# Windowed attention with a gated MLP: two heads' scores in one two-bank tile, and one conditional copy for both

## The chip, the core and the metric

The kernel runs on one core of one Trainium2 chip. The metric is device time in microseconds (us), lower is better; the median of several executions counts. The engines are named as in the profile: PE is TensorE (matrix products and transposes), PEld its loading of weights, DVE is VectorE, ACT is ScalarE, POOL is GpSimd, and SP issues most transfers.

## What is computed

Attention with a few sink columns and a window, then a feed-forward block with a convolution of three taps along the sequence and a gate. All data are float32.

```python
def _attn_ref(q, k, v, n_sink, window):            # (4, 8, 768, 64): batch, heads, rows, head_dim
    scores = (1.0 / np.sqrt(D)) * np.matmul(q, k.transpose(0, 1, 3, 2))
    is_sink = pos[None, :] < int(n_sink)           # n_sink = 4
    rel = pos[:, None] - pos[None, :]
    in_window = (rel >= 0) & (rel < int(window))   # window = 128
    scores = np.where(is_sink | in_window, scores, -1000000000.0)
    a = np.exp(scores - np.max(scores, axis=-1, keepdims=True))
    a = a / (np.sum(a, axis=-1, keepdims=True) + 1e-09)
    return np.matmul(a, v)

def _moe_ref(x, w_in, conv_w, w_out):              # x (4, 768, 512), w_in (512, 1024), w_out (1024, 512)
    h = np.maximum(x @ w_in, 0.0)
    # conv_out: three taps along the sequence, one weight a tap and column, zeros beyond the ends
    return (h * (1.0 / (1.0 + np.exp(-conv_out)))) @ w_out
```

A row of scores has at most 128 window columns and 4 sink columns. Of the 128 rows of one tile, row r needs columns 0 to r of its own tile (the triangle) and columns r+1 to 127 of the tile to its left: together 128 columns.

## The kernel before

**Tiling.** Heads are taken in pairs: 4 batches x 4 pairs = 16 groups g. The 768 rows of a group are 6 tiles t of 128 rows. A step is one tile of one group for both heads j, so there are 96 steps. `banded` (L398) lays the steps out in a list and writes them as a software pipeline: at position i it writes the scores of step i (`scores`, L488), the transposes of step i-1 (`transp`, L526) and, on the third tile of a half, the product with the values (`pv`, L558) of step i-2. Between them it writes pieces of the MLP of the batch before (`fill`) and the preparation of coming keys and queries (`todo`). The first 24 steps, batch 0, multiply in plain float32 (L339); the later ones in two passes of a faster format, a main part and a remainder of the keys (L342, L343).

**The MLP.** It runs in 96 units, 24 a batch. A unit has 12 matmuls into `ph` (L183: 4 blocks of the model width x 3 products), a gate on ACT, DVE and POOL (L190 to L201), and 6 matmuls into `po` (L210). The MLP of a batch needs the attention of all its heads for the rows it takes.

**Order.** The program is built with `schedule_with_timeline_sim=True` (L807): the framework decides from the dependencies, by a plan of its own, in which order each engine gets its instructions. An engine then takes them strictly in that order, so an instruction that waits holds up all those behind it on the same engine.

**A step's scores.** A score tile has 260 columns: 0 to 127 the tile to the left, 128 to 131 the sink columns, 132 to 259 the step's own tile (`P` = 128, `KW` = 132, `SW` = 260). For t = 0 only the last 128 are made. The steps on it:

- PE writes the scores of head 0 into one tile and of head 1 into another (L501 to L505). Both have the tag `sc` with two buffers, one PSUM bank each: head 0's next tile takes the first bank that is free again.
- For t > 0 DVE copies, head by head, the left neighbour's columns over those of the own tile that lie beyond the triangle (L508, a copy under the mask `before`, in place within the bank).
- DVE adds the mask over 132 columns, keeps the row's minimum (the scores are negated) in `sm`, and writes to SBUF (L509, shown as a custom operation and a read of its accumulator). With that the bank is free.
- ACT takes the exponential and its sum, head by head (L512); DVE adds up the sums of both heads (L514) and inverts them (L515); POOL scales (L517). Then PE transposes (L532).

All eight PSUM banks are taken: `h` two, `po` two, `sc` two, `px` one, `pts` one.

Of the kernel before, what the change touches and what calls it, by code (L numbers as in the profile page):

```python
# [10 lines left out]
F32 = mybir.dt.float32  # L11
F32R = mybir.dt.float32r
I32 = mybir.dt.int32
# [4 lines left out]
P = 128  # L18
# [5 lines left out]
KW = P + NS  # L24
SW = 2 * P + NS
# [372 lines left out]
def banded(c):  # L398

    nc = c.nc  # L400
# [6 lines left out]
    ap, ps = A.ap, A.ps  # L407
# [11 lines left out]
    before = cp.tile([P, P], F32, name="before")  # L419
# [64 lines left out]
            asked[0] += 1  # L484

    pts = ps.tile([P, 2, 2, P], F32, name="pts")

    def scores(g, t):  # L488
        s = st[g]
        lo = 0 if t == 0 else (t - 1) * KW  # L490
        mk = m0 if t == 0 else (m1 if t == 1 else m2)
        cols = slice(NS if t == 0 else 0, KW)
        sm = sms[A.tiles % len(sms)]
        A.tiles += 1
        hf, u = divmod(t, 3)
        if u == 0:
            s.pe[hf] = ap.tile([P, 3, 2, KW], F32, tag="pe", name=f"pe{g}_{hf}")
            if t == 0:
                nc.gpsimd.memset(s.pe[hf][:, 0, :, 0:NS], 0.0)
        pe = s.pe[hf][:, u]  # L500
        pcs = [ps.tile([P, SW], F32, tag="sc", name=f"sc{g}_{t}_{j}", bufs=2) for j in range(2)]  # L501
        if t == 0:
            A.scores(s, t, [pc[:, KW:SW] for pc in pcs], lo, lo + P)
        else:
            A.scores(s, t, pcs, lo, lo + SW)  # L505
        for j, pc in enumerate(pcs):
            if t:
                nc.vector.copy_predicated(pc[:, KW:SW], before.bitcast(I32), pc[:, 0:P])  # L508
            nc.vector.tensor_tensor_reduce(out=pe[:, j, cols], in0=pc[:, P:SW][:, cols], in1=mk, op0=ALU.add, op1=ALU.min,  # L509
                                           scale=1.0, scalar=3.0e38, accum_out=sm[:, j:j + 1])  # L510
        for j in range(2):
            nc.scalar.activation(pe[:, j, cols], pe[:, j, cols], AF.Exp, bias=sm[:, j:j + 1], scale=-1.0,  # L512
                                 accum_out=sm[:, 2 + 2 * j:3 + 2 * j])
        nc.vector.tensor_reduce(out=sm[:, 6:8], in_=sm[:, 2:6].rearrange("p (j e) -> p j e", e=2), op=ALU.add, axis=mybir.AxisListType.X)  # L514
        nc.vector.reciprocal(sm[:, 8:10], sm[:, 6:8])  # L515
        for j in range(2):
            nc.gpsimd.tensor_scalar(pe[:, j, cols], pe[:, j, cols], sm[:, 8 + j:9 + j], 1.0, ALU.mult, ALU.mult)  # L517
# [112 lines left out]
    for i in range(NST + D2):  # L630
        if i < NST:
            n, g, t = steps[i]
# [15 lines left out]
        for slot in range(SLOTS):  # L648
            if slot == 0 and i < NST:
                scores(g, t)  # L650
            if slot == 1 and 0 <= i - D1 < NST:
                transp(*steps[i - D1][1:])
            if slot == 2 and 0 <= i - D2 < NST:
                pv(*steps[i - D2][1:])
                if i - D2 + 1 in cuts:
                    while fill:
                        fill.pop(0)()
                    lo, hi, span = cuts[i - D2 + 1]
                    fill = m.pieces(lo, hi)
                    rate = len(fill) / (span - 0.5)  # L660
                    acc = 0.0
            acc += rate / SLOTS
            while acc >= 1.0 and fill:
                fill.pop(0)()
                acc -= 1.0
            while todo and i + (slot + 1) / SLOTS >= todo[0][0]:
                todo.pop(0)[1]()
# [73 lines left out]
def attention_gated_mlp(ctx: ExitStack, tc: tile.TileContext, q, k, v, n_sink, window, w_in, conv_w, w_out, out):  # L741
# [33 lines left out]
    with tc.If(fast == 1) as cmp:  # L775
        with ExitStack() as es:
            c.es = es
            banded(c)
# [32 lines left out]
```

## Time and profile before

| | us |
|---|---|
| median of 3 runs | 489.43 |
| lowest and highest | 487.89, 490.92 |
| the profiled execution | 490.03 |
| its span, first to last instruction | 488.3 |

The profile is of one execution. Busy time of an engine leaves out waits and the instructions that only issue transfers or handle semaphores. Matmuls are pipelined, so their durations overlap. A "group" is all instructions of one line, operation and shape, with their busy time and the mean length of one; behind it stands how long the engine had been idle before them, and what ended that. "Who waited for whom" gives the total, the number of times and the longest. The chain of waits goes back from the last instruction, at each step to what released it. In a timeline a row is start, length, engine, line, operation, output<-inputs, shapes, and a count where neighbours are merged; the time in brackets is the idle time before it and its releaser.

By span: the first 20 us load and set up, the first 24 steps run up to about 97 us, the other 72 from 100.0 to 402.5 us (L509's first and last start are 10.3 and 402.5 us), and after 412 us only the MLP of the last batch is left.

### The profile page before, as it was taken

To read this page: it belongs to the slowest core of one execution; us is meant where nothing else is said; L and a number is where in the kernel's file an instruction comes from. 1 tells how busy PE (TensorE), PEld (TensorE's weight loads), DVE (VectorE), ACT (ScalarE), POOL (GpSimd) and SP (SyncE) were. 2 spreads that over 40 slices of the span, in tenths; PEclk is the share of its full clock that TensorE was granted. 3 is DMA by queue.
4 is the path that set the end of the run, shared out by engine and by line. 5 is a ranking of instruction groups with operands and counts; after the bars stand their busy time and mean duration, and the time that the engine had idled before them with its cause. 6 is when DMAs were issued, how large, how long until landed. Compare 5 with 4: busy or idle time off the path is not lost.

```text
span 488.3 us, 10470 instructions
## 1 busy us (share of the span) xinstructions
PE 457.4 (94%) x3149; PEld 389.7 (80%) x3149; DVE 348.4 (71%) x1212; ACT 340.5 (70%) x1086; POOL 312.7 (64%) x614
## 2 busy tenths in 40 slices
PE   2887798899999999999999999999999999999995
PEld 2555477688889888888888888888888888999993
DVE  4798989957968777786677585886675665656553
ACT  3887858778878977786877786876776754545451
POOL 3584796867976867684758577685764564344441
PEclk9988989999999999999999999999999999999998
DMA  5778653537234132334132332324021100101011
GB/s 147 211 229 212 172 168 79 126 85 188 67 72 116 61 83 66 87 96 99 60 77 58 85 81 60 70 63 98 24 55 33 44 3 0 44 2 44 1 44 53
DMA packets 87307, 41.03 MB, mean 84 GB/s; under 512 B 80160, under 2 KB 80184, under 8 KB 87240
## 3 DMA queue, kind: packets, MB, share of 16 engines
q1 hardware_dynamic: 87096, 39.99, 31.5%
q8 instruction: 28, 0.46, 0.4%
q14 instruction: 39, 0.32, 0.2%
q10 hardware_dynamic: 144, 0.26, 0.2%
HBM read 27.60 MB, written 6.29 MB: 69 GB/s over the span
## 4 chain that ended last, share of the span: by engine, by line
PE 80%; DVE 7%; DMA 3%; issue 3%; ACT 2%; POOL 2%; SPq 1%; DVEq 0%; ACTq 0%; POOLq 0%
PE po L210 27%; PE ph L183 26%; PE px L573 8%; PE sc L342 4%; PE pts L532 4%; PE sc L343 3%; PE px L576 2%; PE tq L276 2%; PE tk L294 2%; PE sc L339 2%; POOL pe L517 1%; DVE sc L508 1%; DMA wi_1r<-in_moe_w_in_dram 1%; DVE pe L509 1%; DVE stm L113 1%
## 5 line engine op out<-in xcount | busy, mean ns | idle before, releaser
L210 PE MATMUL po<-woH,g 128*128 128x512 f32 x384 | 142.0, 409 | 1.2 <-POOL g L200 1.0
L183 PE MATMUL ph<-xH,wiH 128*128 128x258 f32 (+1 forms) x384 | 112.2, 292 | 1.2 <-ACT X L255 1.2
L183 PE MATMUL ph<-xH,wiL 128*128 128x258 f32 (+1 forms) x384 | 109.0, 284 | 0.0
L183 PE MATMUL ph<-xL,wiH 128*128 128x258 f32 (+1 forms) x384 | 108.8, 284 | 0.0
L517 POOL TENSOR_SCALAR pe<-pe,sm 128x132 f32<-128x132 f32 (+1 forms) x192 | 82.8, 442 | 34.9 <-DVE sm L515 27.2
L512 ACT ACTIVATE pe<-pe,sm 128x132 f32<-128x132 f32 (+1 forms) x192 | 77.5, 406 | 15.8 <-DVE sm L509 14.7
L200 POOL TENSOR_SCALAR g<-t 128x256 fp32r<-128x256 f32 x96 | 42.2, 439 | 70.7 <-DVE t L198 50.8
L195 DVE SCALAR_TENSOR_TENSOR t<-hb,cw,t 128x256 f32<-128x256 f32 x96 | 54.0, 562 | 36.6 <-ACT t L194 36.1
L201 POOL TENSOR_TENSOR g<-t,g 128x256 fp32r<-128x256 f32 x96 | 75.2, 784 | 5.6
L210 PEld LDWEIGHTS po<-woH,g 128*128 128x128 f32 x384 | 68.7, 189 | 11.6 <-POOL g L200 2.6
L183 PEld LDWEIGHTS ph<-xH,wiH 128*128 128x128 f32 x384 | 73.0, 190 | 5.5 <-ACT X L255 1.6
L210 PE MATMUL po<-woL,g 128*128 128x512 f32 x192 | 76.4, 398 | 0.0
L183 PEld LDWEIGHTS ph<-xH,wiL 128*128 128x128 f32 x384 | 72.9, 190 | 2.1
L183 PEld LDWEIGHTS ph<-xL,wiH 128*128 128x128 f32 x384 | 72.8, 190 | 0.7
L197 ACT ACTIVATE t<-t 128x256 f32<-128x256 f32 x96 | 40.1, 418 | 33.8 <-DVE t L196 33.4
L198 DVE SCALAR_TENSOR_TENSOR t<-t,hb 128x256 f32<-128x256 f32 x96 | 47.5, 494 | 20.1 <-ACT t L197 19.0
L508 DVE COPY_PREDICATED sc<-before,sc 128x128 f32<-128x128 int32 x160 | 45.6, 291 | 22.6 <-PE sc L343 19.1
L509 DVE CUSTOM_DVE_ANT_0 pe<-sc,m 128x132 f32<-128x132 f32 (+1 forms) x192 | 54.0, 288 | 10.3 <-PE sc L343 7.8
L190 ACT ACTIVATE hb<-ph 128x258 f32<-128x258 f32 (+1 forms) x96 | 37.0, 386 | 31.4 <-PE ph L183 30.7
L536 POOL TENSOR_SCALAR_AFFINE_SELECT pT<-pT 128x256 f32<-128x256 f32 x80 | 38.2, 477 | 31.4 <-ACT pT L534 31.1
L196 DVE SCALAR_TENSOR_TENSOR t<-hb,cw,t 128x256 f32<-128x256 f32 x96 | 54.1, 564 | 4.1
L194 ACT ACTIVATE t<-hb,cw 128x256 f32<-128x256 f32 x96 | 49.2, 513 | 7.7 <-POOL g L201 3.9
(124 smaller groups left out, 930.2 us busy)
## 6 DMA issues: line engine op xcount, KB each, us to landing
raw<-in_q_dram SPq DMA_DIRECT2D x64, 96.0 KB
raw<-in_k_dram SPq DMA_DIRECT2D x64, 96.0 KB
out_dram<-stm SPq DMA_DIRECT2D x23, 256.0 KB
kk<-kk SPq DMA_DIRECT2D x24, 198.0 KB
vraw<-in_v_dram SPq DMA_DIRECT2D x24, 192.0 KB
wi_0r<-in_moe_w_in_dram SPq DMA_DIRECT2D x2, 512.0 KB
wi_1r<-in_moe_w_in_dram SPq DMA_DIRECT2D x2, 512.0 KB
wi_2r<-in_moe_w_in_dram SPq DMA_DIRECT2D x2, 512.0 KB
```

The lines of the kernel that those rows point to most:

```text
L183: nc.tensor.matmul(u.h[:, 0:W], w[:, cc, ff * P:(ff + 1) * P], x[:, cc, t0:t1], start=(i == 0), stop=(i == len(prods) - 1))
L194: nc.scalar.mul(a, prev, cw[:, 0, ff:ff + 1])
L195: nc.vector.scalar_tensor_tensor(out=e, in0=this, scalar=cw[:, 1, ff:ff + 1], in1=a, op0=ALU.mult, op1=ALU.add)
L196: nc.vector.scalar_tensor_tensor(out=a, in0=nxt, scalar=cw[:, 2, ff:ff + 1], in1=e, op0=ALU.mult, op1=ALU.add)
L198: nc.vector.scalar_tensor_tensor(out=a, in0=e, scalar=1.0, in1=this, op0=ALU.add, op1=ALU.mult)
L200: nc.gpsimd.tensor_scalar(u.g[:, 0], a, 1.0, 1.0, ALU.mult, ALU.mult)
L201: nc.gpsimd.tensor_tensor(out=u.g[:, 1], in0=a, in1=f(u.g[:, 0]), op=ALU.subtract)
L210: nc.tensor.matmul(po[:, 0:c.DM], u.g[:, a, tt * P:(tt + 1) * P], w[:, ff, :], start=(ff == 0 and i == 0), stop=(ff == NFF - 1 and i == 2))
L508: nc.vector.copy_predicated(pc[:, KW:SW], before.bitcast(I32), pc[:, 0:P])
L509: nc.vector.tensor_tensor_reduce(out=pe[:, j, cols], in0=pc[:, P:SW][:, cols], in1=mk, op0=ALU.add, op1=ALU.min, scale=1.0, scalar=3.0e38, ...
L512: nc.scalar.activation(pe[:, j, cols], pe[:, j, cols], AF.Exp, bias=sm[:, j:j + 1], scale=-1.0, accum_out=sm[:, 2 + 2 * j:3 + 2 * j])
L517: nc.gpsimd.tensor_scalar(pe[:, j, cols], pe[:, j, cols], sm[:, 8 + j:9 + j], 1.0, ALU.mult, ALU.mult)
```

## The change

The two score tiles of a step are no longer taken from a pool of two buffers. One tile of two banks, `scs`, is allocated once before the loop and used by every step; head j always has bank j. The two conditional copies become one instruction over both banks: 128 partitions x 2 x 128 columns, the mask read twice through a stride of zero. It stands after both heads' score matmuls and before both masking passes.

```diff
     pts = ps.tile([P, 2, 2, P], F32, name="pts")
+    scs = ps.tile([P, 2, 512], F32, name="sc")
 
     def scores(g, t):
...
         pe = s.pe[hf][:, u]
-        pcs = [ps.tile([P, SW], F32, tag="sc", name=f"sc{g}_{t}_{j}", bufs=2) for j in range(2)]
+        pcs = [scs[:, j, 0:SW] for j in range(2)]
         if t == 0:
             A.scores(s, t, [pc[:, KW:SW] for pc in pcs], lo, lo + P)
         else:
             A.scores(s, t, pcs, lo, lo + SW)
+        if t:
+            nc.vector.copy_predicated(scs[:, :, KW:SW], before.bitcast(I32).rearrange("p (o k) -> p o k", o=1).to_broadcast([P, 2, P]),
+                                      scs[:, :, 0:P])
         for j, pc in enumerate(pcs):
-            if t:
-                nc.vector.copy_predicated(pc[:, KW:SW], before.bitcast(I32), pc[:, 0:P])
             nc.vector.tensor_tensor_reduce(out=pe[:, j, cols], in0=pc[:, P:SW][:, cols], in1=mk, op0=ALU.add, op1=ALU.min,
                                            scale=1.0, scalar=3.0e38, accum_out=sm[:, j:j + 1])
```

## The prediction

> **What bounds the kernel now.** I read the profiled execution first as a whole and then by stages, because a share of busy time averages over stages with different limits. First the head of the page, the busy times and the chain of work that ended last:
>
> ```profile
> span 488.3 us, 10470 instructions
> ...
> PE 457.4 (94%) x3149; PEld 389.7 (80%) x3149; DVE 348.4 (71%) x1212; ACT 340.5 (70%) x1086; POOL 312.7 (64%) x614
> ...
> PE 80%; DVE 7%; DMA 3%; issue 3%; ACT 2%; POOL 2%; SPq 1%; DVEq 0%; ACTq 0%; POOLq 0%
> ```
>
> TensorE (PE) is busy for 457.4 of 488.3 us and makes up 80% of the chain; VectorE (DVE) makes up 7%, some 34 us. Where those are is seen in the busy times of four stages (columns: stretch, its length, then PE, PEld, DVE, ACT and POOL busy with their counts, the granted clock, the DMA share and GB/s):
>
> ```profile
> 0.00:20.00 20.00, 10.26 (x45) 7.95 (x46) 12.18 (x53) 10.95 (x31) 8.02 (x30) 1.00 0.62 153
> 20.00:100.00 80.00, 66.24 (x390) 49.78 (x389) 70.32 (x241) 61.81 (x201) 61.10 (x102) 0.91 0.62 167
> 100.00:412.00 312.00, 310.44 (x2283) 269.32 (x2282) 226.30 (x845) 233.29 (x777) 213.04 (x434) 1.00 0.29 71
> 412.00:488.00 76.00, 70.42 (x437) 62.64 (x436) 39.64 (x74) 34.48 (x80) 30.50 (x50) 0.98 0.08 30
> ```
>
> From 100 to 412 us PE is busy for 310.4 of 312 us: nothing that shortens DVE can shorten that stage. From 20 to 100 us PE is busy for 66.2 of 80 us, at a granted clock of 0.91, and DVE for 70.3 of 80 us. The same split in the chain of waits, for 20 to 100 us and then for 100 to 412 us:
>
> ```profile
> by line: issue 11.9%; PE sc L339 9.5%; POOL pe L517 5.8%; PE po L210 5.6%; DVE sc L508 5.1%; DVE pe L509 5.1%; DVE stm L113 4.1%; DVE t L196 4.0%; PE ph L183 3.9%; DMA raw<-in_k_dram 3.5%; PE px L573 3.4%; DVE woL L122 3.0%; ACT pe L512 2.7
> ```
>
> ```profile
> by line: PE ph L183 29.3%; PE po L210 29.1%; PE px L573 11.7%; PE sc L342 5.9%; PE sc L343 5.2%; PE pts L532 5.0%; PE tq L276 3.1%; PE px L576 2.7%; PE tk L294 2.5%; SPq L395 1.0%; issue 0.7%; DMA vsr<-sinkl 0.6%; PE tk L554 0.5%; ACT stm L
> ```
>
> The copy (L508) holds 5.1% of the first window's 80 us on the chain, 4.1 us, and the masking pass (L509) as much; in the second window neither is among the lines shown and PE lines have nearly all. What is left for the last stage, after 412 us:
>
> ```profile
> L210 PE MATMUL po<-woH,g 128*128 128x512 f32 x104 | 36.4, 396 | 0.0
> ...
> L183 PE MATMUL ph<-xH,wiH 128*128 128x258 f32 (+1 forms) x92 | 26.0, 283 | 0.0
> ```
>
> One unit of the gated MLP has four matmuls of the second row's kind and four of the first's, so 23 units of the first half and 26 of the second are left: this is the last batch, whose input is the attention that has just ended. So PE goes from one filled stage into another, and attention ends about when the older MLP work runs out.
>
> **The change, part by part.** The two score tiles of a step become the two banks of one tile that lives through the whole kernel (no cost by itself: two banks before, two after). 160 copies of 128 columns become 80 copies of 2 x 128. The masking passes, exponentials, sums and scalings stay.
>
> *The copy's length.* Groups by form:
>
> ```profile
> L508 DVE COPY_PREDICATED sc<-before,sc 128x128 f32<-128x128 int32 x160 | 45.6, 291 | 22.6 <-PE sc L343 19.1 <-PE sc L339 2.0
> L509 DVE CUSTOM_DVE_ANT_0 pe<-sc,m 128x132 f32<-128x132 f32 x160 | 45.1, 288 | 1.9 <-DVE sc L508 0.2
> ...
> L351 DVE TENSOR_TENSOR xL<-px,xH 128x384 fp32r<-128x384 f32 x32 | 17.7, 552 | 7.3 <-ACT xH L350 7.0
> ```
>
> A copy of 128 columns takes 291 ns, a masking pass over 132 columns 288 ns, a subtraction of 384 columns that also reads a matmul result 552 ns: (552 - 288) / (384 - 132) = 1.05 ns per column, and some 150 ns whatever the width. A copy of 256 columns is then 291 + 128 x 1.05 = 425 ns, against 2 x 291 = 582 ns: 157 ns less for a step. No row shows a predicated copy of that width, nor one whose mask is read twice by a zero stride. If nothing is saved it is 582 ns; lower than 425 ns no row supports. I take 425, because three rows of different operations lie on one line.
>
> *How much of that is DVE's own time.* In the early stage:
>
> ```profile
> 24.00 1.14 PE L339 MATMUL sc<-kk,X 128*128 128x260 f32 x4 [0.17 <-DVE sm L509]
> ...
> 24.75 0.29 DVE L508 COPY_PREDICATED sc<-before,sc 128x128 f32<-128x128 int32 x1 [0.59 <-PE sc L339]
> ...
> 25.56 0.29 DVE L508 COPY_PREDICATED sc<-before,sc 128x128 f32<-128x128 int32 x1
> ...
> 25.76 0.69 DVE L113 SCALAR_TENSOR_TENSOR stm<-wi_2r,stm 128x512 int32<-128x512 int32 x1
> ```
>
> The copy at 25.56 lasts 0.29 us, but the next operation, which does not depend on it, starts at 25.76, 0.20 us later. Two copies then hold the queue for 0.40 us and the merged one for 0.20 + 0.13 = 0.33: 0.07 us less a step by this row, 0.16 by the durations. The Trainium skill, page "VectorE: DVE Perf Modes", section "The DRAIN you can't avoid", says that the next Vector operation does not start until the pipe of the one before has emptied. By it the whole 0.16 us would count each time, and the sum below would be about 1 us lower; the row at 25.76 does not agree, at least where the next operation reads nothing that the copy wrote.
>
> Copies by stage:
>
> ```profile
> 0.00:100.00 100.00, 11.41 (x40) 0.93 0.62 164
> 100.00:412.00 312.00, 34.19 (x120) 1.00 0.29 71
> ```
>
> 40 of the 160, 20 steps, lie before 100 us: 20 x 0.07 to 20 x 0.16 is 1.4 to 3.2 us of DVE time. The 35 or so after 20 us would hold 35 x 0.20 = 7.0 us of the queue, and 4.1 us of copies are on the chain: 0.58 of it. So the gain is 0.58 x 1.4 = 0.8 to 0.58 x 3.2 = 1.9 us; I take 1.0, near the lower end, because the successors I looked at mostly start early. The 120 copies after 100 us save 60 x 0.07 to 60 x 0.16 = 4 to 10 us of DVE time that lies beside PE, worth nothing.
>
> *The longer wait.* One copy needs both heads' scores. In the early rows four score matmuls take 1.14 us, 0.57 us a head: the first head's copy starts at 24.75, when only its own are done. After the change the first pass can end up to 0.57 + 0.13 = 0.70 us later than now, when the second head's matmuls come at once behind the first's. The second head's pass is not later where DVE is the one that is late. Behind the waiting copy on DVE stand the two passes, then weight narrowing and the gate's work; behind the first pass stand its exponential on ACT and the next step's first score matmul, which writes the same bank. Sum, reciprocal and scaling of the step need both heads already now. How often PE waits for a bank:
>
> ```profile
> PE sc L339 <- DVE sm L509: 4.3, 7, 1.7
> ...
> PE sc L339 <- DVE sm L515: 1.8, 2, 1.1
> ```
>
> L339 makes the scores of the first 24 steps, all before 100 us: nine waits there and 6.1 us in all (two of them the view puts down to the reciprocal, which came last). If each of the nine grew by 0.70 us it would cost 6.3 us; if the second head sets the pace, each grows by no more than the copy's extra 0.13 us, 1.2 us in all; and if DVE's lighter load reaches those passes, nothing. I take 1.2: the step's end hangs on the second head, and the bank of the second head comes free no later than now.
>
> After 100 us the same wait falls on a PE that has other work, if that work stands next in its order:
>
> ```profile
> 148.21 0.28 PE L342 MATMUL sc<-kk,X 128*128 128x260 f32 x1
> ...
> 148.44 0.29 PE L183 MATMUL ph<-xH,wiH 128*128 128x260 f32 x1
> ```
>
> ```profile
> 147.94 0.30 DVE L508 COPY_PREDICATED sc<-before,sc 128x128 f32<-128x128 int32 x1 [1.07 <-PE sc L343]
> ```
>
> ```profile
> 282.31 0.54 DVE L508 COPY_PREDICATED sc<-before,sc 128x128 f32<-128x128 int32 x2
> 282.76 1.14 DVE L300 TENSOR_TENSOR kk<-tk,kk 64x384 fp32r<-64x384 f32 x2
> ```
>
> The copy at 147.94 had waited for a second head's scores; at 148.21 come the next step's first head's. The merged copy could start at 147.94 and the first pass would end at 147.94 + 0.43 + 0.29 = 148.66, so the matmul at 148.21 would have to come 0.45 us later, behind MLP matmuls such as the one at 148.44. The order on the engines is planned, not that of the code: at 282.31 two copies run in a row, with key preparation (L300) behind them, where the code has copy, pass, copy, pass. So the new waits will be planned around, and the cover is MLP matmuls. If the old order were kept, 60 steps x 0.45 = 27 us would be lost; I do not count that, but it says what the cover is worth. There is room in a step:
>
> ```profile
> L342 PE MATMUL sc<-kk,X x144: 220/287/391, 100.0 to 401.1; 128*128 128x260 f32 x120, 128*128 128x128 f32 x24
> ```
>
> 72 steps between 100.0 and 401.0 us are 4.2 us a step; both heads' matmuls, the merged copy and two passes are about 0.23 + 0.40 + 0.43 + 0.58 = 1.6 us (the first head's pair, 148.21 to 148.44; the second's pair to its end, 0.12 + 0.28; copy; two passes). DVE already idles there for scores, and will idle longer:
>
> ```profile
> DVE sc L508 <- PE sc L343: 19.1, 36, 1.2
> ```
>
> These 19.1 us fall in a stage where DVE is busy for 226 of 312 us, so up to 60 x 0.23 = 14 us more fits.
>
> *The sum.* 490.03 us (the time of the profiled execution, its span of 488.3 and 1.7 around it) - 1.0 + 1.2 = 490.2. That execution lies 0.6 us above the median of 489.43, so against the median the forecast is 489.6 us.
>
> **The rivals.** Within 1%, or 4.9 us, is about what a measurement of this kernel cannot tell from no change.
>
> *Faster: DVE's relief frees the early stage.* DVE is 88% busy from 20 to 100 us and the clock is at 0.91. If all 3.2 us are on the path and PE, with fewer gaps, gets half of the missing 9% of its 66.2 us back, 3.0 us, the time is 489.4 - 3.2 - 3.0 = 483.2. For it: 4.1 us of copies on the chain. Against: "issue", POOL and DMA take more of that window than the copy, and they stay.
>
> *Slower: the banks no longer alternate.* Now one head's bank is filled while the other's is worked on; then both are held until the common copy is done. If every one of the nine waits grows by the full 0.70 us, the time is 489.4 + 6.3 = 495.7. It decides when those waits in the early stage pass about 11 us in place of 6.1. For it: DVE starts the first copy 0.57 us before the second head's scores are there. Against: the bank waits are only 6.1 of the 14 us that PE idles between 20 and 100 us, and most steps there have other work between. The Trainium skill, page "PSUM — Partial Sum Buffer", section "PSUM bank collisions raise a hardware error", says that TensorE writing and VectorE reading or writing must not touch one bank at the same time. By that rule, too, the merged copy shuts both banks to PE while it runs; the row at 24.00, whose matmul waits for the pass, agrees.
>
> *No saving: the merged copy costs as much as two,* 582 ns. Then the 1.0 us of gain is gone and the first pass is later by 0.29 instead of 0.13: 490.03 + 9 x 0.29 - 0.6 = 492.0, still within 1%.
>
> **How the numbers follow.** The forecast, hidden within a few microseconds, 0.60; its own range is 487 to 492.5. The faster rival 0.15, the slower 0.17, no saving 0.08. A new planned order can move the early stage by a microsecond or two either way, which the ranges take in. Faster by over 1% is the faster rival, 0.15; slower by over 1% the slower one, 0.17; within 1% the rest, 0.68. The range of 485 to 496 holds the forecast, the case of no saving and the slower rival, and leaves out most of the faster one.
>
> **What would show it.** Right: 80 copies of 128 x 256 at about 0.43 us; DVE busy for some 12 us less (336 in place of 348); PE still busy for 310 of 312 us in the middle; about as much PE idle time from 20 to 100 us; attention ending near 412 us with 23 units left. Wrong: PE idle between 100 and 412 us, the last scores well after 402 us, or waits of score matmuls for L509 that grow past 11 us (slower); a clock near 1.00 and the first 24 steps done before 94 us (faster); copies at 0.58 us (no saving). A middle stage that is no longer full of PE work would overturn the whole argument.

## The result: slower by 2.6%, the later scores 13 us late

The changed kernel takes 502.27 us (median of 4 runs, 501.89 to 503.09), the kernel before beside it 489.52 (4 runs, 487.89 to 490.92): a ratio of 1.026, 95% interval 1.0233 to 1.0287. The forecast was 489.6 us with a range of 485 to 496.

The page of the changed kernel, its span and busy times:

```profile
span 501.3 us, 10326 instructions
...
PE 468.0 (93%) x3149; PEld 394.1 (79%) x3149; DVE 342.8 (68%) x1132; ACT 340.3 (68%) x1086; POOL 314.4 (63%) x614
```

DVE does less: 342.8 us in place of 348.4. PE is busy for 468.0 in place of 457.4 us with the same 3149 matmuls. Its work has not grown: the ends of pipelined matmuls are modelled, and seem to take in some of the waiting. The stages, with the same limits as in the prediction:

```profile
20.00:100.00 80.00, 65.60 (x358) 48.11 (x358) 65.50 (x206) 60.01 (x186) 56.80 (x90) 0.89 0.58 162
100.00:412.00 312.00, 308.63 (x2227) 265.11 (x2227) 220.22 (x788) 229.08 (x774) 211.17 (x429) 0.99 0.29 73
```

From 20 to 100 us DVE is busy for 65.5 in place of 70.3 us and PE for 65.6 in place of 66.2, but PE starts 358 matmuls there in place of 390. So both engines stand more: less gets done in the same time. The first matmuls of the later steps' scores (columns: shortest, median and longest in ns, first and last start):

```profile
L342 PE MATMUL sc<-kk,X x144: 220/283/420, 113.3 to 414.7; 128*128 128x260 f32 x120, 128*128 128x128 f32 x24
```

Before, these ran from 100.0 to 401.1 us, now from 113.3 to 414.7. The whole 13 us seem to have been lost in the first 24 steps, and the later ones to take what they took (301.4 for 301.1 us). That reading leaves out what else PE got done meanwhile. Here are the busy times up to the start of the later steps, of all instructions and then of the first MLP product alone (L183, PE and PEld), in the changed kernel and then in the kernel before:

```profile
0.00:113.26 113.26, 89.20 (x484) 66.17 (x485) 82.96 (x277) 78.94 (x242) 74.20 (x140) 0.92 0.58 156
...
0.00:113.26 113.26, 15.02 (x96) 13.47 (x96) 0.92 0.58 156
```

```profile
0.00:100.01 100.01, 76.51 (x434) 57.75 (x435) 82.50 (x293) 72.76 (x230) 69.14 (x132) 0.93 0.62 164
...
0.00:100.01 100.01, 12.31 (x84) 11.21 (x84) 0.93 0.62 164
```

PE has started 50 matmuls more by then. Twelve are of the first MLP product, which is one unit: 8 units are begun in place of 7. The others are 8 of the second MLP product, 22 products with the values, and 8 transposes. Matmuls overlap, so their durations can't be added up; from one matmul's start to the next one's they take 0.08 to 0.25 us, by kind, in the later steps of the kernel before, and the 50 are then about 6.4 us of work (an estimate). So the first 24 steps lost about 13.3 - 6.4 = 6.9 us, and the later 72, which had that much less to do and still took as long, lost about 0.3 + 6.4 = 6.7 us. Two experiments below (e3, e4) find nearly the same two parts.

Who waited for whom on PE (total, times, longest, in us) in the changed kernel, and the one row on the transposes and POOL in the kernel before:

```profile
PEld pts L534 <- POOL pe L519: 15.9, 23, 3.6
...
PE pts L534 <- POOL pe L519: 9.6, 12, 3.2
...
PEld sc L339 <- DVE sm L511: 5.0, 6, 1.6
...
PE sc L339 <- DVE sm L511: 3.3, 4, 1.4
...
PEld sc L342 <- DVE sm L511: 1.8, 3, 1.1
...
PE sc L342 <- DVE sm L511: 1.2, 2, 0.9
```

```profile
PEld pts L532 <- POOL pe L517: 2.6, 3, 1.3
```

In this trace the idle time on PE for these waits lies within that on PEld (weight loads), so the two are not added. The waits of the scores for the pass (L339 and L342 on L511) are 4.5 us on PE and about 7 on PEld; before, nearly all of them were on PE, with 6.1 us in the two rows of L339 in the prediction and 6.5 in all. So they have hardly grown. What is new is the wait of the transposes for POOL's scaling: 2.6 us on PEld before (L532 on L517), now (L534 on L519) 15.9 us on PEld, of which 9.6 show on PE. PE takes its instructions in the planned order, so a step whose scaling comes late is seen where PE next needs it, not where the delay arose. The delay arises in the steps' own loop. The early steps in the changed kernel and then before, in a timeline:

```profile
22.71 1.14 PE L339 MATMUL sc<-kk,X 128*128 128x260 f32 x4 [0.54 <-DVE sm L511]
...
23.89 0.43 DVE L508 COPY_PREDICATED sc<-before,sc 128x256 f32<-128x256 int32 x1 [0.97 <-PE sc L339]
...
24.36 0.29 DVE L511 CUSTOM_DVE_ANT_0 pe<-sc,m 128x132 f32<-128x132 f32 x1
...
24.58 0.29 DVE L511 CUSTOM_DVE_ANT_0 pe<-sc,m 128x132 f32<-128x132 f32 x1
...
24.93 0.71 PE L339 MATMUL sc<-kk,X 128*128 128x128 f32 x4 [0.97 <-DVE sm L511]
```

```profile
18.71 0.71 PE L339 MATMUL sc<-kk,X 128*128 128x260 f32 x2
...
19.45 0.29 DVE L508 COPY_PREDICATED sc<-before,sc 128x128 f32<-128x128 int32 x1 [0.36 <-PE sc L339]
...
19.58 0.60 PE L339 MATMUL sc<-kk,X 128*128 128x260 f32 x2
...
19.90 0.30 DVE L509 CUSTOM_DVE_ANT_0 pe<-sc,m 128x132 f32<-128x132 f32 x1 [0.15 <-DVE sc L508]
...
20.35 1.33 PE L339 MATMUL sc<-kk,X 128*128 128x260 f32 x4
...
20.55 0.29 DVE L509 CUSTOM_DVE_ANT_0 pe<-sc,m 128x132 f32<-128x132 f32 x1
...
21.84 0.46 PE L339 MATMUL sc<-kk,X 128*128 128x128 f32 x2
```

Changed: four score matmuls from 22.71, the copy only at 23.89, when both heads' are done, two passes, and the next step's first matmul at 24.93, just behind the second pass. This step takes 2.2 us, with PE and DVE in strict turn. Before: the first head's copy starts at 19.45 while the second head's matmuls (19.58) are still ahead; the first head's pass is done at 20.2, and the next step's matmuls start at 20.35, 0.2 us before the second head's pass starts (20.55). From 18.71 to 20.35 and to 21.84 a step takes 1.6 and 1.5 us. In these stretches the steps follow one another closely. Most steps take longer in both kernels: from the first score at 9.4 us on, the first 24 took 3.8 us each on average before and 4.3 now, the work done early included.

### The profile page after: what moved, and what is told of

Same layout as the page of the kernel before. It is cut to its first block, busy times and chain, and to the rows that moved or that the text cites. A ratio compares the mean times of both kernels' runs of the same rounds, so it can differ in the third digit from the quotient of the medians.

```text
span 501.3 us, 10326 instructions
## 1 busy us (share of the span) xinstructions
PE 468.0 (93%) x3149; PEld 394.1 (79%) x3149; DVE 342.8 (68%) x1132; ACT 340.3 (68%) x1086; POOL 314.4 (63%) x614
## 4 chain that ended last, share of the span: by engine, by line
PE 83%; DVE 8%; DMA 3%; POOL 2%; issue 2%; ACT 1%; SPq 1%; DVEq 0%; POOLq 0%; ACTq 0%
PE ph L183 27%; PE po L210 26%; PE px L575 10%; PE pts L534 4%; PE sc L342 4%; PE sc L343 3%; PE px L578 3%; PE tq L276 2%; PE sc L339 2%; PE tk L294 2%; POOL pe L519 2%; DVE stm L113 1%; DVE stm L114 1%; DMA wi_2r<-in_moe_w_in_dram 1%; DVE pe L511 1%
## 5 line engine op out<-in xcount | busy, mean ns | idle before, releaser
L519 POOL TENSOR_SCALAR pe<-pe,sm 128x132 f32<-128x132 f32 (+1 forms) x192 | 86.5, 461 | 45.5 <-DVE sm L517 33.0
L183 PE MATMUL ph<-xH,wiH 128*128 128x258 f32 (+1 forms) x384 | 112.9, 294 | 0.0
L183 PE MATMUL ph<-xH,wiL 128*128 128x258 f32 (+1 forms) x384 | 110.5, 288 | 0.0
L183 PE MATMUL ph<-xL,wiH 128*128 128x258 f32 (+1 forms) x384 | 109.8, 286 | 0.0
L195 DVE SCALAR_TENSOR_TENSOR t<-hb,cw,t 128x256 f32<-128x256 f32 x96 | 57.1, 595 | 42.1 <-ACT t L194 41.5
L201 POOL TENSOR_TENSOR g<-t,g 128x256 fp32r<-128x256 f32 x96 | 74.0, 771 | 5.7
L183 PEld LDWEIGHTS ph<-xH,wiH 128*128 128x128 f32 x384 | 73.5, 191 | 4.1 <-issue 0.9
L183 PEld LDWEIGHTS ph<-xH,wiL 128*128 128x128 f32 x384 | 73.6, 192 | 2.2
L183 PEld LDWEIGHTS ph<-xL,wiH 128*128 128x128 f32 x384 | 73.6, 192 | 0.8
L538 POOL TENSOR_SCALAR_AFFINE_SELECT pT<-pT 128x256 f32<-128x256 f32 x80 | 39.9, 499 | 31.7 <-ACT pT L536 30.1
L198 DVE SCALAR_TENSOR_TENSOR t<-t,hb 128x256 f32<-128x256 f32 x96 | 46.1, 481 | 17.2 <-ACT t L197 16.2
L196 DVE SCALAR_TENSOR_TENSOR t<-hb,cw,t 128x256 f32<-128x256 f32 x96 | 54.7, 570 | 4.1
L575 PE MATMUL px<-pT,vraw 128*64 128x256 f32 (+1 forms) x448 | 53.7, 358 | 0.8 <-POOL pT L540 0.8
L511 DVE CUSTOM_DVE_ANT_0 pe<-sc,m 128x132 f32<-128x132 f32 (+1 forms) x192 | 49.2, 287 | 6.7 <-PE sc L343 3.9
```

The costliest lines, as they stand in the source:

```text
L183: nc.tensor.matmul(u.h[:, 0:W], w[:, cc, ff * P:(ff + 1) * P], x[:, cc, t0:t1], start=(i == 0), stop=(i == len(prods) - 1))
L195: nc.vector.scalar_tensor_tensor(out=e, in0=this, scalar=cw[:, 1, ff:ff + 1], in1=a, op0=ALU.mult, op1=ALU.add)
L196: nc.vector.scalar_tensor_tensor(out=a, in0=nxt, scalar=cw[:, 2, ff:ff + 1], in1=e, op0=ALU.mult, op1=ALU.add)
L198: nc.vector.scalar_tensor_tensor(out=a, in0=e, scalar=1.0, in1=this, op0=ALU.add, op1=ALU.mult)
L201: nc.gpsimd.tensor_tensor(out=u.g[:, 1], in0=a, in1=f(u.g[:, 0]), op=ALU.subtract)
L575: nc.tensor.matmul(px[D * j:D * j + D, P * (lo - first):P * (hi - first) + P], s.v[:, kt, j, :], pT[:, j, cols], start=(kt == tiles[0]), s ...
```

## The experiments

All are told as ratio to the kernel before in the same set of runs, and in us of that set (the kernel before had 489.5 to 490.6).

| run | score tiles, copies | median us | ratio (95%) | later 72 steps' first and last score |
|---|---|---|---|---|
| before | rotating, 2 | 489.52 | 1 | 100.0, 401.1 |
| after | one of two banks, 1 | 502.27 | 1.0260 (1.0233 to 1.0287) | 113.3, 414.7 |
| e1 | one of two banks, 2 | 523.24 | 1.0673 (1.0655 to 1.0691) | 124.1, 433.9 |
| e2 | two fixed of one bank, 2 | 488.68 | 0.9970 (0.9958 to 0.9981) | 99.9, 399.8 |
| e3 | as before early, as after late | 495.16 | 1.0108 (1.0087 to 1.0129) | 100.4, 407.5 |
| e4 | as after early, as before late | 496.52 | 1.0119 (1.0103 to 1.0136) | 113.6, 408.3 |
| e5 | as after, waits by bank | 495.70 | 1.0120 (1.0097 to 1.0142) | 105.9, 406.3 |
| e6 | e2, released together | 493.53 | 1.0076 (1.0052 to 1.0101) | 105.3, 402.9 |
| e7 | e2, entered together | 499.56 | 1.0204 (1.0179 to 1.0228) | 105.3, 409.1 |
| e8 | before without the copies | 484.86 | 0.9908 (0.9877 to 0.9939) | 97.1, 394.2 |

**The tile or the copy (e1, e2).** e1 keeps the one tile and takes the two copies back; e2 takes two copies and two tiles that stay, head j always in bank j.

e1 against the changed kernel, and e2 against the kernel before:

```diff
-        if t:
-            nc.vector.copy_predicated(scs[:, :, KW:SW], before.bitcast(I32).rearrange("p (o k) -> p o k", o=1).to_broadcast([P, 2, P]),
-                                      scs[:, :, 0:P])
         for j, pc in enumerate(pcs):
+            if t:
+                nc.vector.copy_predicated(pc[:, KW:SW], before.bitcast(I32), pc[:, 0:P])
```

```diff
+    sc2 = [ps.tile([P, 512], F32, name=f"sc{j}") for j in range(2)]
...
-        pcs = [ps.tile([P, SW], F32, tag="sc", name=f"sc{g}_{t}_{j}", bufs=2) for j in range(2)]
+        pcs = [sc2[j][:, 0:SW] for j in range(2)]
```

> One tile of two banks as after the change, but the two copies of the kernel before. Theory: the loss comes from the tile, because waits are laid on a tile as a whole, so that the next step's first score matmul waits for both heads' passes and the first head's copy for both heads' matmuls. Then this takes 502 to 505 us, no less than the change's 502.3, and the second head's score matmul again waits for nothing. Rival, the merged copy: the loss comes from one copy needing both heads' scores. Then this takes 488 to 492 us.

> Two tiles of one bank each, allocated once and used by every step, head j always in tile j; two copies as before the change. Theory (waits by tile): 488 to 492 us, as before the change, since each head's matmul waits for its own pass alone. Rival, the fixed place: if it is the loss of the rotating buffers, or only another planned order, 496 to 503 us.

The same two banks and the same two copies: 523.24 us in one tile, 488.68 in two. So the copies' merging is not what costs; on the one tile it brings 21 us (523.24 to 502.27). That the banks no longer rotate costs nothing, as e2's theory had it. The tile costs, and by more than was expected for e1. Why is seen in the built programs, in the order of PE's instructions for one early step and what each waits for (the framework sets these waits):

```
changed kernel
L339 MATMUL sc<-kk_175,X_180 128x260 [waits DVE_49]
L339 MATMUL sc<-kk_175,X_180 128x260
e2
L339 MATMUL sc_174<-kk_176,X_181 128x260 [waits DVE_49]
L533 MATMUL pts<-ident,pe_0_208 128x128 [waits Pool_49]
L339 MATMUL sc_175<-kk_176,X_181 128x260 [waits DVE_49]
```

With two tiles each head's matmul has its own wait for DVE. With one tile only the first has one, and the second needs none, because the first has waited for the release of the whole tile: for the second head's pass. DVE's side is alike in e1: its first copy waits for PE, its second only for DVE's own work, the first head's pass, so the wait for both heads' matmuls falls on the first copy. The framework guards a tile, not a bank. In e1's timeline one step then takes 4.65 us (36.01 to 40.66) and the next 1.94:

```profile
36.01 2.10 PE L339 MATMUL sc<-kk,X 128*128 128x260 f32 x4
...
38.16 0.30 DVE L509 COPY_PREDICATED sc<-before,sc 128x128 f32<-128x128 int32 x1 [0.96 <-PE sc L339]
...
38.36 0.69 DVE L122 TENSOR_TENSOR woL<-stm,woH 128x512 fp32r<-128x512 f32 x1
...
40.31 0.29 DVE L510 CUSTOM_DVE_ANT_0 pe<-sc,m 128x132 f32<-128x132 f32 x1
...
40.66 0.71 PE L339 MATMUL sc<-kk,X 128*128 128x128 f32 x4
...
42.60 1.14 PE L339 MATMUL sc<-kk,X 128*128 128x260 f32 x4 [1.23 <-DVE sm L510]
```

Four instructions of DVE lie between one step's scores and the next one's, from 38.16 on, and they do not stand close together: other work of DVE, such as the weight preparation of L122, comes between them, and they take 2.44 us where four by 0.29 us are 1.2. After the merging there are three.

**Where it is lost (e3, e4).** The change in the later 72 steps alone (e3) and in the first 24 alone (e4): the pool of score tiles is closed and opened again at the first step of the second batch.

```diff
+        if (g, t) in ((0, 0), (NPAIR, 0)):
+            pair[0] = open_scores(g >= NPAIR)          # one tile of two banks if late == LATE, else two rotating tiles
+        scs = pair[0]
...
-        if t:
+        if t and scs is not None:
```

> Batch 0 (the first 24 steps) with two rotating tiles and two copies, the other 72 steps with one tile and one copy. Theory (the loss arises in the first 24 steps, where PE has little other work): 488 to 492 us, and step 24 starts near 100 us. Rival, that the later steps lose too, each a little: 495 to 502 us.

> The reverse: the first 24 steps with one tile and one copy, the other 72 with two rotating tiles and two copies. Theory (the loss arises in the first 24 steps): 499 to 504 us, and step 24 starts near 113 us. Rival, that the later steps lose too: 491 to 497 us.

Neither theory holds, and both rivals do: each half loses about 1.1%, and 1.08 + 1.19 = 2.3% is most of the 2.6 of the whole. The first matmuls of the later steps in e3 and in e4:

```profile
L343 PE MATMUL sc<-kk,X x144: 221/283/391, 100.4 to 407.5; 128*128 128x260 f32 x120, 128*128 128x128 f32 x24
```

```profile
L343 PE MATMUL sc<-kk,X x144: 220/283/392, 113.6 to 408.3; 128*128 128x260 f32 x120, 128*128 128x128 f32 x24
```

In e3 the later steps take 307.1 in place of 301.1 us, with the first 24 as before: 6.0 us lost where PE was busy for 310.4 of 312. In e4 step 24 starts at 113.6, with the same work done early as in the changed kernel, and the later steps take 294.7 us: 6.4 us less than before, which is what the 50 matmuls were estimated at. So the last scores come 6.4 us later in e3 and 7.2 in e4, together the 13.6 of the changed kernel. That confirms the split above, and also that a unit less to carry does not by itself slow the later steps.

**Entry or release (e5, e6, e7).** The one tile does two things: the first copy and pass wait for both heads' matmuls (entry), and the next step's first matmul waits for both passes (release). e5 is the changed kernel with the release by bank: the common copy must still wait for both heads, but each head's matmuls wait only for that head's pass (and for t = 0, without a copy, the first pass only for the first head). e6 and e7 are e2 with one of the two waits added.

```diff
+        if A.freed is not None:                          # e5: A.made = score matmuls, A.freed = the passes before
+            for j in range(2):
+                wait_also(A.made[j][0], A.freed[j])
+            for x in A.made[0]:
+                no_wait(x, A.freed[1])
...
+        if RELEASE and A.freed is not None:              # e6: A.freed = the second head's pass
+            wait_also(A.made[0][0], A.freed)
...
+            if ENTRY and j == 0:                         # e7: one[0] = the first head's copy (t = 0: its pass)
+                wait_also(one[0], A.made[1][1])
```

> The change, one tile and one copy, but with the waits laid by bank: a head's score matmul waits for its own head's pass of the step before and no longer for the other head's, and at t = 0 the first pass no longer for the second head's matmul. Theory (what costs time is that the tile is one unit for the waits): 487 to 492 us, like two fixed tiles, 488.7. Rival (the merged copy's own wait for both heads' scores costs as well): 494 to 500 us.

> Two fixed tiles and two copies (488.7 us), with one wait added: the first head's score matmul of the next step also waits for the second head's pass, so that both banks come free together. The first head's copy still starts on its own scores. Theory (one tile costs 33 us through its waits, and most of it through this one): 505 to 523 us. Rival (it is the copy's wait for both heads' matmuls that costs): 489 to 496 us.

> Two fixed tiles and two copies, with the other wait added: the first head's copy (at t = 0 its pass) also waits for the second head's score matmuls; the banks come free singly. Theory (most of the loss comes from the joint release): 489 to 496 us. Rival: 500 to 520 us.

e5 falls to the rival's range: of the 12.7 us some 6.6 go with the release by tile (502.27 to 495.70; by the ratios 1.4 of the 2.6 points), and nearly as much stays. e6's and e7's theory had the order of the two the wrong way round: over e2 the common release costs 1.1% (4.8 us), the common entry 2.3% (10.9 us), and both together with two copies, e1, 34.6 us, more than twice their sum. As I read it, a wait on one side is taken up by the freedom on the other, and with both PE and DVE work in turn; this is not shown. e1 also has a wait that e6 and e7 lack, that of the second head's copy for the first head's pass, and every one of these kernels gets a planned order of its own, which no run held fixed. In e7 the copies are still two; the merged copy under nearly the same waits, e5, is 3.9 us faster. So the merged copy seems to be worth something, and its entry wait costs more than that: e5 is still 7.0 us slower than e2.

Which wait costs the time can't be read off the places where PE stands. The weight loads' waits for the pass and for the scaling, in e6 and then in e7:

```profile
PEld sc L342 <- DVE sm L520: 9.8, 11, 2.9
...
PEld pts L546 <- POOL pe L531: 6.1, 14, 1.0
```

```profile
PEld sc L342 <- DVE sm L520: 10.7, 7, 4.1
...
PEld pts L546 <- POOL pe L531: 5.3, 11, 0.9
```

The two are nearly alike, while one loses 4.8 us over e2 and the other 10.9.

**What the copies are worth at all (e8).** The two copies are left out, and with them the left neighbour's columns.

```diff
-            if t:
-                nc.vector.copy_predicated(pc[:, KW:SW], before.bitcast(I32), pc[:, 0:P])
```

> The kernel before without the conditional copy (the left neighbour's columns are left out), so with 160 DVE instructions fewer: a bound for what any cheaper copy can bring. Theory (copies matter only in the first 100 us, 58% of them on the chain): 485 to 489 us. Rival (DVE's load holds up the whole early stage, and the clock comes back): 478 to 484 us.

484.86 us, just under the theory's range: with no copy at all the gain would be 0.9%, 4.5 us. With the score tiles of the kernel before, no shorter copy could bring more than some such amount.

**PE's order at the transposes (e9 to e16).** If the entry wait shows as PE standing at the transposes, a step more between scores and transposes should take it away. D1 and D2 are how many positions behind the scores the transposes and the value products are written. With them alone (e9, e10, e12), the load of the next values stands ahead of products that still need the old ones, so that in the first batch the values of another pair of heads enter the product; the instructions are the same. In e13 to e16 that load is called at the end of its position, and the computation is the whole one.

```diff
-    D1, D2 = 1, 2
+    D1, D2 = 2, 3
...
-            if n + 1 < len(jobs) and (t % 3 == 2 if n < 2 * NPAIR else t == 3):     # e13 to e16: moved behind the loop over slots
-                values(n + 1)
```

> The changed kernel with its transposes written one step later and its products with the values two positions after them as before (D1, D2 = 2, 3 for 1, 2). Theory: the loss is seen where PE, in its fixed order, comes to the transposes before POOL has scaled the step (9.6 us of waits on PE and 15.9 us on PEld in the changed kernel, 2.6 us before); with one more step between, most of these waits go and the time falls from 502 to 490-496 us. Rival: the step's period is set by the scores' own loop (matmuls, common copy, two passes, next matmuls), the waits at the transposes only show the delay; then the time stays at 500-505 us and the waits come back at the score matmuls.

> The kernel before with the same two numbers (D1, D2 = 2, 3). Theory: there are only 2.6 us of waits at its transposes, so it gains at most 1-2 us: 487-491 us. Rival: the later transposes help or hurt whatever the score tiles are (a longer pipeline, a new planned order): over 3 us either way, and then the run of the changed kernel with them is read against this one.

> Two fixed tiles of one bank, two copies, and the later transposes (D1, D2 = 2, 3). Theory: its waits are by bank already, so the later transposes give it no more than they give the kernel before: 486-490 us. Rival: 3 us or more below the two fixed tiles alone, which would make it the fastest version with the whole computation.

> The changed kernel with D1, D2 = 2, 3 and the call that loads the next values moved behind the products of its position (in e9 that load came ahead of products that still needed the old values, so that the first batch took those of another pair). Theory: the values' place matters little, the time is that of e9, 495-499 us, some 5 us below the changed kernel and 6-9 us above the kernel before: the transposes hold PE up for under half of the loss, the scores' own loop for the rest. Rival: the later load of the values costs the early stage more than 2 us: 500-505 us.

> One tile and one common copy with waits by bank (as e5, 495.7 us), and the later transposes and values of e13. Theory: the transposes' part and the part of the waits by tile are two different ones, so they add: 495.7 - 5 = 489-492 us. Rival: both are the same idle time of PE: 494-497 us.

> Two fixed tiles, two copies, and the later transposes and values of e13. Theory: as e12, 487-489 us, 0.994-0.998 of the kernel before. Rival: the later load of the values takes that back: 489.5-493 us.

> The kernel before with the later transposes and values of e13. Theory: as e10, 487-489.5 us. Rival: the later load of the values takes that back: 490-493 us.

| score tiles, copies | as written | later transposes (e9, e10, e12) | and the values behind (e13 to e16) |
|---|---|---|---|
| before: rotating, 2 | 1 | 0.9956 (488.14 us) | 1.0029 (490.57 us) |
| e2: two fixed, 2 | 0.9970 | 0.9956 (488.20 us) | 1.0058 (492.27 us) |
| e5: one tile, 1, by bank | 1.0120 | not run | 1.0067 (492.56 us) |
| after: one tile, 1 | 1.0260 | 1.0134 (496.92 us) | 1.0231 (500.52 us) |

The later load of the values costs 0.7 to 1.0% (second column to third), which the rivals of e13, e15 and e16 allowed for; so rows are compared within a column. Against the kernel before of the same column, the changed kernel's loss goes from 2.6 to 1.8 (e9, e10) or 2.0% (e13, e16), and that of waits by bank from 1.2 to 0.4% (e14, e16). e9 lies just above its theory's range; e10 and e12 came as their theories had it; e13, e15 and e16 fell to their rivals. Each ratio is known to 0.15 to 0.3 points. So the later transposes recover 0.6 to 0.8 points whatever the release, most of what e5 had left, and only part of the changed kernel's loss: the release by tile still costs 500.52 - 492.56 = 8.0 us with them. e14's theory, that the two parts add, is nearer than its rival (492.56; 489 to 492 and 494 to 497). The two fixed tiles gained nothing from later transposes (e12) or lost (e15), so that e14 stands within 0.3 us of them. PE's waits at the scores and transposes in e5 and e14:

```profile
PE pts L552 <- POOL pe L537: 6.5, 6, 2.3
PE sc L341 <- DVE sm L519: 4.7, 4, 2.6
```

```profile
PE sc L341 <- DVE sm L519: 6.9, 6, 3.6
PE pts L552 <- POOL pe L537: 2.4, 3, 1.3
```

With the later transposes PE stands 2.4 us for the scaling in place of 6.5. So the two parts are different ones: the later transposes take away most of what e5 had left, and not what the release by tile costs. That the common entry acts by delaying the scaling, and the common release by holding up PE's next scores, fits this but is not shown, as the rows of e6 and e7 look alike.

**The fastest whole version (e11).** e2 once more, in five rounds:

> The two fixed tiles of one bank with two copies, once more, in five rounds. Theory: it was 0.997 of the kernel before and stays between 0.995 and 0.999, a gain of 1 to 2 us. Rival: that gain was between two runs of the same time: 0.999-1.001.

489.21 us for 490.55, a ratio of 0.9972 (0.9962 to 0.9983): a gain of 0.3%, seen twice, by two tiles that stay in place of two that rotate. No run with the merged copy was faster than the kernel before.

## Why the prediction was wrong, step by step

- **What bounds the kernel:** right that the middle is PE's; wrong in what was drawn from it, that a delay of DVE's steps after 100 us costs nothing. e3 shows 6.0 us lost there. The changed kernel from step 24 to the end of attention, as a stage and then the waits in it for the pass and the scaling:

```profile
113.26:426.42 313.16, 309.90 (x2239) 266.66 (x2238) 221.36 (x784) 228.29 (x768) 210.17 (x427) 0.99 0.27 67
```

```profile
PEld sc L342 <- DVE sm L511: 1.8, 3, 1.1
...
PEld pts L534 <- POOL pe L519: 1.6, 5, 0.5
...
PE sc L342 <- DVE sm L511: 1.2, 2, 0.9
...
PE pts L534 <- POOL pe L519: 0.5, 2, 0.3
```

  PE is busy for 309.9 of 313.2 us there, and no wait carries the loss: 1.2 and 0.5 us on PE, 1.8 and 1.6 on its weight loads. From one matmul's start to the next one's the transposes took 13.4 us (146 matmuls) where they took 11.5 (148) from 100.0 to 412.3 us before, the transposes of keys and sinks (`tk`) 10.8 for 8.5 (91 each), but the scores 37.9 for 41.3 (288 each). The granted clock is 0.99 in place of 1.00, but e3, which loses 6.0 us there too, has 1.00 from 100.39 to 413 us. How the 6 us divide among small parts was not settled. The prediction's sign for this stage, PE busy for 310 of 312 us, came true and still did not show the loss: PE's modelled busy time is not the work it gets done.
- **The copy's length:** right, 423 ns on average for 425:

```profile
L508 DVE COPY_PREDICATED sc<-before,sc 128x256 f32<-128x256 int32 x80 | 33.9, 423 | 26.0 <-PE sc L343 20.8 <-PE sc L339 4.9
```

- **DVE's saving:** 0.07 us a step by the row at 25.76, 0.16 by the durations, was the right pair of bounds. The copies' durations fell from 45.6 to 33.9 us, DVE's busy time by 348.4 - 342.8 = 5.6 us, which is 80 x 0.07. That time takes in every other change on DVE too, but it lies at the lower bound, and the 336 us named as a sign followed the upper one. The Trainium skill, page "VectorE: DVE Perf Modes", section "The DRAIN you can't avoid", from which the prediction quoted that the next operation waits for an empty pipe, adds that a next operation that is not held starts earlier. With that addition the row at 25.76, 0.20 us after the start of a copy of 0.29 us, agrees.
- **The tile "no cost by itself: two banks before, two after":** wrong, and with it **the longer wait**, the step that failed. It was written that each wait grows by the copy's extra 0.13 us because "the bank of the second head comes free no later than now". That took the waits to be laid by bank. They are laid by tile: the next step's first matmul waits for both passes, where it had waited for one. Nine waits of the early stage were priced, 1.2 us, at most 6.3; but every step carries the two common waits, and where steps follow closely the loop went from 1.5 or 1.6 to 2.2 us. Against the 1.2 us, release by tile measured 6.6 us (after less e5), entry and copy together 7.0 (e5 less e2).
- **The cover after 100 us:** it was assumed that the new waits "will be planned around". The planned order did change: PE makes both heads' scores in one run, where two tiles let transposes stand between. But the plan can't remove a wait that lies on the tile. That one MLP unit less was left as cover is not the reason: e3 has the unit and loses 6.0 us after step 24.
- **The slower rival** had the mechanism, both banks held until the common copy is done, and too small a price (6.3 us), since it counted only existing waits. Its sign was wrong too: the waits of scores for the pass did not pass 11 us, they are about 7 on PEld (4.5 on PE) for 6.5 before, while the waits at the transposes grew from 2.6 to 15.9 us on PEld and came up on PE with 9.6. The rule quoted with it, from the Trainium skill, page "PSUM — Partial Sum Buffer", section "PSUM bank collisions raise a hardware error", asks for a guard by bank, or finer; the guard by tile is coarser, and its surplus is the 6.6 us that e5, guarded by bank, gets back.
- **The signs:** last scores near 402 us: no, 414.7. 80 copies at about 0.43 us: yes. As much PE idle time from 20 to 100 us: yes, 14.4 us for 13.8, with 358 matmuls begun in place of 390.

## What to carry to other kernels

When two buffers become one, look first at what the synchronisation guards: two banks in one tile are held and released together, and each consumer of one half waits for both. Price such a wait for every turn of the loop, not for the waits that are seen today, and look for it where the next engine in strict order needs the result, which need not be where the wait is laid. A merged instruction that saves 0.07 us of an engine's time a step is not worth a handover in which two engines stop overlapping; if it is made, give each half its own tile or its own waits, and check what the joint entry holds up.

## What was not expected of the hardware

The same 160 copies in the same two banks cost 34.6 us more as one tile than as two (e1, e2), while the two common waits alone cost 4.8 and 10.9 us (e6, e7): here the costs of the waits did not add up. PE's granted clock fell with it, seen from 20 to 100 us in e1:

```profile
20.00:100.00 80.00, 61.29 (x292) 42.58 (x291) 59.40 (x199) 51.59 (x160) 47.55 (x79) 0.83 0.50 145
```

0.83, with PE busy for 61.3 us, where the changed kernel had 0.89 and 65.6, and the kernel before 0.91 and 66.2. Where PE stood more its granted clock was lower, so part of the lost time may be the clock's; how much was not measured apart.
